# Four array tiles for the 47-point products of an FFT, mixing and feed-forward kernel on one core: units in doubles, a shared ring of PSUM banks, other distances between operands

## The chip, the cores and the metric

One core of a Trainium2 chip. The metric is the device time of one launch in microseconds (us). The kernel before takes 2804.76 us, the median of 3 runs from 2804.42 to 2804.91.

## What is computed

```python
X = np.fft.rfft(x, axis=1)                      # x: 8 x 3008 x 256, float32
Yr = Xr @ w_r - Xi @ w_i + b_r                  # w_r, w_i: 256 x 256
Yi = Xr @ w_i + Xi @ w_r + b_i
Y = soft(Yr) + 1j * soft(Yi)                    # sign(v) * max(|v| - 0.01, 0)
y = np.fft.irfft(Y, n=3008, axis=1)
gate = sigmoid(y @ w_gate)                      # 24064 tokens, 256 -> 1536
out = (gate * (y @ w_val)) @ w_out              # 1536 -> 256
```

## The kernel before

The length 3008 is 47 times 64. The forward transform of a sequence has two steps. Step A is a 47-point product over the rows, with the table `fa` as stationary operand. It goes out to the DRAM tensor `zd`, and step B reads `zd` back for a 64-point product (`fwd_b`, tile `pb`). Then come mixing (`mix`, tiles `pm` and `pm3`), the soft threshold and the inverse 64-point product (`inv_b`, tile `pi`), whose result goes to DRAM as `vd`. The inverse of step A (`load_v`, `inv_a`, tile `pia`) is the 47-point product back: here the data `vf` is stationary and the table `fb_sb` moves.

Step A takes two rows of the 64 at once: `fa` holds the 47-point table twice, interleaved, so that one matmul contracts 94 partitions into 96 (`product_a`, tile `pa`). A call of `fwd_a` handles 4 column positions of both halves with two matmuls of 512 columns. The inverse does the same with 96 partitions and 94 moving columns: a unit `u` is four matmuls. There are 128 units, 16 in each of 8 sequences, and `fwd_a` or its half-sized form `half_a` covers the 16 matmuls of a sequence. These products, step B and the table products of the first sequence are plain float32. The trace shows each such matmul as two weight loads and two matmuls; the order of the program shows it once. The rest splits its operands into two float32r parts, with three matmuls for a product.

The feed-forward part is direct for the first 9 blocks of 512 tokens: `ffn1` makes `pg` and `pv` with 12 matmuls each step, `ffn2` makes `po` with 6. It uses `yth`, `ytl`, `hh` and `hl` as moving operands and `w1h`, `w1l`, `w2` as stationary ones. All later tokens are written to DRAM as `yd`, and 19 pairs of blocks of 512 go through a Strassen scheme: `half` makes seven products in the banks `pa` to `pd` (line 661), four of which open a bank and three of which add to one, and `second` makes 12 matmuls into `po` between them (lines 636 to 638).

Four stages follow each other: the transform of sequence 0 and the start of 1 (to 100 us), the first direct block beside the weights' conversion and step A of sequences 2 and 3 (to 185 us), the other eight direct blocks with all the rest of the transforms merged in (to 1064.5 us), and the Strassen scheme. In the third stage the unit lists in `side` are dealt out between the steps of `ffn`, by weights that stand for TensorE time (1.7 for a `fwd_a`, 0.65 for an inverse unit); a scheduler then sets the order on each engine. Sequences 4 to 7 have step A there (`step_a` in `fft_units`), and 122 of the 128 inverse units are run there. PSUM's eight banks are 3 for the transforms (`FFT_BANKS`), 3 for `ffn1` (`L1_BANKS`) and 2 for `po`.

Of the kernel before, what the change touches and what calls it, by code (L numbers as in the profile page):

```python
# [27 lines left out]
FFT_BANKS, L1_BANKS, L2_BANKS = 3, 3, 2  # L28

NF2K, NR2K, NLD, NST, NBIG, NMF, NME, NVF, NVO, NHH, NSG, NYF = 5, 4, 3, 3, 5, 3, 2, 3, 1, 3, 2, 3  # L30
# [4 lines left out]
PRE = 2  # L35
# [30 lines left out]
def _tables(seq):  # L66
# [3 lines left out]
    fa = np.zeros((R2, 2, NK2, 2, 2))  # L70
    fb = np.zeros((NK2, 2, 2, 128))
    for j in range(2):
        fa[:, j, :, 0, j] = c
        fa[:, j, :, 1, j] = -s
        fb[:, 0, j, j:2 * R2:2] = c.T / seq
        fb[:, 1, j, j:2 * R2:2] = -s.T / seq
    fa = fa.reshape(2 * R2, 2 * NQ)
    fb = fb.reshape(2 * NQ, 128).astype(np.float32)
# [27 lines left out]
    return {"mf": mf, "mi": mi, "mis": mis, "fa": fa.astype(np.float32), "fb": fb}  # L106
# [3 lines left out]
def tile_fft_mix_ffn(ctx: ExitStack, tc, x, w_r, w_i, b_r, b_i, w_one, w_out, mf, mi, mis, fa, fb, out):  # L110
# [9 lines left out]
    PT = 2 * R2  # L120
    UT = 2 * PT
    NU = B * H // 2
# [9 lines left out]
    edge.tile([P, 8], F32, name="edge")  # L132
# [6 lines left out]
    psl = ctx.enter_context(tc.tile_pool(name="psl", bufs=3, space=bass.MemoryType.PSUM))  # L139
    psfs = ExitStack()  # L140
    psf = psfs.enter_context(tc.tile_pool(name="psf", bufs=FFT_BANKS, space=bass.MemoryType.PSUM))

    def bank(name, tag="fft", bufs=FFT_BANKS):
        return (psf if tag == "fft" else psl).tile([P, 512], F32, tag=tag, bufs=bufs, name=name)
# [7 lines left out]
    fa_sb = cw.tile([2 * R2, 2 * NQ], F32, name="fa_sb")  # L152
# [9 lines left out]
    vv = [v.rearrange("q (j h) c -> (q j) h c", j=2) for v in vd]  # L162
# [18 lines left out]
    def fwd_a(b, h):  # L181

        xf = held["x", b, h]
        for i in range(2):
            at = slice(2 * i, 2 * i + 2)
            product_a(xf[:2 * R2, at], xf[:2 * NQ, at], nc.vector.tensor_copy if b < 2 and i else nc.scalar.copy)
# [9 lines left out]
    def half_a(b, h):  # L196

        xi = held.pop(("xh", b, h))[:2 * R2]
        az = p2.tile([P, 2, D], F32, tag="st", bufs=NST, name="azh")[:2 * NQ]
        product_a(xi, az, nc.scalar.copy)  # L200
        nc.gpsimd.dma_start(zv[b][:, 2 * h:2 * h + 2], az)


# [5 lines left out]
    def load_mi(q, full, later=False):  # L209
        t = p2.tile([P, 2, 2, P], F32 if full else F32R, tag="mi_sb", bufs=NME, name="mi_sb")  # L210
        if full:
# [16 lines left out]

    def load_b(b, q):
# [91 lines left out]
    def load_v(u):  # L321
        own = 2 * UT <= u * UT < T0
        vf = p3.tile([P, 2, D], F32, tag="vo" if own else "vf", bufs=NVO if own else NVF, name="vf")[:2 * NQ]
        b, h = divmod(2 * u, H)
        nc.sync.dma_start(vf, vv[b][:, h:h + 2])
        held["v", u] = vf
# [3 lines left out]
    def split_y(c, at, n, y):  # L330
        if c not in yts:
            yts[c] = [p3.tile([P, CT, CW], F32R, name=t) for t in ("yth", "ytl")]
# [4 lines left out]
    def inv_a(u):  # L337
        vf = held.pop(("v", u))
        pa = bank("pia")[:, :CT * UT].rearrange("p (c h k) -> p c h k", c=CT, h=2)
# [3 lines left out]
        py = pa.rearrange("p c h k -> p c (h k)")  # L343
        lo = u * UT
        n = 0
        if lo < T0:
            c, at = divmod(lo, CW)
            n = min(UT, CW - at)
        if 0 < n < UT and lo + n < T0:
            t = p3.tile([P, 3 * P], F32, name="carry", bufs=1)[:, :CT * UT].rearrange("p (c k) -> p c k", c=CT)[:, :, :UT - n]  # L350
            nc.scalar.copy(t, py[:, :, n:])
            held["carry", c + 1] = t, UT - n
        if n:
            split_y(c, at, n, py[:, :, :n])
        if lo + UT > T0:
            t = result("yf")
            t = t[:, :CT * (UT - n)].rearrange("p (c k) -> p c k", c=CT)
            nc.scalar.copy(t, py[:, :, n:])
            nc.sync.dma_start(yd[:, :, lo + n - T0:lo + UT - T0], t)
# [3 lines left out]

    def carry(c):
        if ("carry", c) in held:
            t, n = held.pop(("carry", c))
            split_y(c, 0, n, t)

# [26 lines left out]
    def ffn1(c, f):  # L395
        yth, ytl = yts[c]
        pg, pv = bank("pg", "l1", L1_BANKS), bank("pv", "l1", L1_BANKS)
# [44 lines left out]
    def fft_units(bs, ms):  # L442


        aa = [(b, h) for b in bs for h in range(R1 // 8)]
        units = []

        def step_a(i):
            if i == 0:
                for k in range(min(PRE, len(aa))):  # L450
                    load_a(*aa[k])
            if i + PRE < len(aa):
                load_a(*aa[i + PRE])
            fwd_a(*aa[i])
            store_a(*aa[i])
# [23 lines left out]
        first = [(1.7, lambda i=i: step_a(i)) for i in range(len(aa))]  # L479
# [6 lines left out]
    def ffn_units():  # L486
# [3 lines left out]
        def own(c):  # L490

            return range(-(-c * CW // UT), -(-(c + 1) * CW // UT))

        for c in range(1, NPL):
            at = (c - 1) * NF
            for i, u in enumerate(own(c)):
                todo.setdefault(at + (0, 3, 6)[i], []).append(lambda u=u: load_v(u))
                todo.setdefault(at + (3, 6, 9)[i], []).append(lambda u=u: inv_a(u))
            todo.setdefault(at + 1, []).append(lambda c=c: carry(c))

        def unit(n):
            c, f = seq[n]
            if n == 0:
                for i, u in enumerate(own(0)):
                    if i == 1:
                        w = w1h[:, 0].rearrange("p i t n -> p (i t n)")
                        keep_warm(bank("warm", "l1", L1_BANKS), w[:, :P], w, WARM_V)
                    inv_a(u)
# [160 lines left out]
    def half(k, extra):  # L669
# [76 lines left out]
    ebias = cw.tile([P, 16], F32, name="ebias")[:, :1]  # L746
    fb_sb = const.tile([2 * NQ, P], F32, name="fb_sb")
# [113 lines left out]
    with tc.manual_schedule():  # L861
# [22 lines left out]
        for q in range(NP + 2):  # L884
# [7 lines left out]
            if q == 3:  # L892
                nc.sync.dma_start(fb_sb, fb)
# [58 lines left out]
    def inverse(g):  # L952

        us = [u for b in g for u in range(b * H // 2, (b + 1) * H // 2) if u >= u0]
# [10 lines left out]
        return [(0.0, begin)], [(0.65, lambda i=i: go(i)) for i in range(len(us))]  # L965
# [26 lines left out]
    for j in range(NF, len(ffn)):  # L992
# [5 lines left out]
        while side and (acc >= side[0][0] or j >= (part if len(side) > n_last else end) - 1):  # L998
# [12 lines left out]
            if not side:  # L1011
                psfs.close()
                psg = ctx.enter_context(tc.tile_pool(name="psg", bufs=1, space=bass.MemoryType.PSUM, reuse_waits="tile"))
# [16 lines left out]

    open_banks(0)
    first_product = products(0)
    a, b, c, d = banks[0]
    for o, xn, wn in (a, "a11", "b11"), (d, "s3", "t3"), (b, "s2", "t2"), (c, "s1", "t1"):
# [61 lines left out]
```

## Time and profile before

| | us |
|---|---|
| median of 3 runs | 2804.76 |
| span of the profiled execution | 2802.9 |
| TensorE (PE) matmuls, busy | 2786.4 (99%) |
| PE weight loads, busy | 2304.7 (82%) |
| VectorE (DVE) | 2084.6 (74%) |
| ScalarE (ACT) | 1311.1 (47%) |
| GpSimd (POOL) | 713.1 (25%) |

The profiled execution's own time is not listed apart from its span; the median lies 1.9 us above the span, which holds what goes on before the first and after the last instruction. A busy time is the union of the durations of an engine's instructions. Matmuls overlap each other in the array, so the duration of one is longer than the distance from its start to the start of the next, and only the latter says what a matmul costs in a stream.

### The profile page before, as it was taken

The numbers are of one execution on the slowest core, as the hardware profiler recorded it, in microseconds if no ns is written. First come the engines' busy times: TensorE is split into PE (matmuls) and PEld (weight loads), VectorE is DVE, ScalarE is ACT, GpSimd is POOL, SyncE is SP. The second block draws the span as 40 slices with busy tenths as digits, with TensorE's granted clock in tenths as the row PEclk, the third lists the DMA queues.
The fourth block names the chain that finished last, engine by engine and source line by source line (L and its number), as shares of the span: only waits on it lengthen the run. The fifth ranks groups of instructions, "written<-read, shape, count | busy, mean of one in ns | idle before, by whom it ended". The sixth has DMA issues, their size and how long they took to land.

```text
span 2802.9 us, 38251 instructions
## 1 busy us (share of the span) xinstructions
PE 2786.4 (99%) x13896; PEld 2304.7 (82%) x13896; DVE 2084.6 (74%) x3109; ACT 1311.1 (47%) x2276; POOL 713.1 (25%) x638
## 2 busy tenths in 40 slices
PE   9999999999999999999999999999999999999999
PEld 6778888888899888888888888888888888888887
DVE  5777788767787536777777777777777777777776
ACT  4664544545455444444444444444444444444443
POOL 0211010224100002333433333333333243333321
PEclk9999999999999999999999999999999999999999
DMA  9866545666554661000000000000000000000000
GB/s 296 258 216 193 172 144 151 199 186 193 168 153 144 187 188 36 31 16 16 31 31 28 3 31 31 31 16 16 31 31 16 15 31 31 31 2 30 31 16 16
DMA packets 173469, 241.01 MB, mean 86 GB/s; under 512 B 14592, under 2 KB 124896, under 8 KB 173280
## 3 DMA queue, kind: packets, MB, share of 16 engines
q1 hardware_dynamic: 163776, 214.93, 25.2%
q0 software_dynamic: 9408, 23.60, 2.6%
q8 instruction: 110, 1.80, 0.3%
q14 instruction: 79, 0.65, 0.1%
q10 hardware_dynamic: 96, 0.04, 0.0%
HBM read 134.17 MB, written 104.33 MB: 85 GB/s over the span
## 4 chain that ended last, share of the span: by engine, by line
PE 96%; DVE 2%; DMA 1%; ACT 0%; issue 0%; SPq 0%; DVEq 0%; ACTq 0%
PE pd L661 11%; PE pa L661 11%; PE pc L661 11%; PE po L636 8%; PE po L638 7%; PE po L637 7%; PE pm L273 6%; PE pb L661 5%; PE pia L342 4%; PE pa L178 3%; PE pb L239 3%; PE pg L401 2%; PE pg L403 2%; PE pg L402 2%; PE po L429 2%; PE pv L401 2%
## 5 line engine op out<-in xcount | busy, mean ns | idle before, releaser
L636 PE MATMUL po<-hh,w 128*128 128x512 f32 x912 | 360.1, 395 | 0.0
L638 PE MATMUL po<-hl,w 128*128 128x512 f32 x912 | 358.0, 393 | 0.0
L720 POOL TENSOR_TENSOR c<-c,c 128x512 f32<-128x512 f32 x114 | 148.3, 1301 | 820.8 <-DVE c L716 630.7
L637 PE MATMUL po<-hh,w 128*128 128x512 f32 x912 | 355.9, 390 | 0.0
L661 PE MATMUL pa<-a,w1h 128*128 128x512 f32 x912 | 284.0, 393 | 0.0
L661 PE MATMUL pc<-s,w1h 128*128 128x512 f32 x912 | 282.6, 391 | 0.0
L716 DVE TENSOR_TENSOR c<-u,pc 128x512 f32<-128x512 f32 x228 | 156.8, 688 | 106.3 <-PE pc L661 99.1
L691 DVE TENSOR_TENSOR u<-u,pb 128x512 f32<-128x512 f32 x228 | 155.4, 681 | 90.5 <-PE pb L661 63.5
L608 ACT CAST hh<-v 128x512 fp32r<-128x512 f32 x114 | 70.8, 621 | 305.9 <-DVE v L701 305.9
L638 PEld LDWEIGHTS po<-hl,w 128*128 128x128 f32 x912 | 171.0, 188 | 41.0
L661 PEld LDWEIGHTS pc<-s,w1h 128*128 128x128 f32 x912 | 171.1, 188 | 38.6
L637 PEld LDWEIGHTS po<-hh,w 128*128 128x128 f32 x912 | 171.2, 188 | 38.3
L661 PEld LDWEIGHTS pa<-a,w1h 128*128 128x128 f32 x912 | 171.3, 188 | 37.5
L636 PEld LDWEIGHTS po<-hh,w 128*128 128x128 f32 x912 | 171.3, 188 | 36.8
L612 POOL TENSOR_TENSOR hl<-c,hh 128x512 fp32r<-128x512 f32 x114 | 153.1, 1343 | 186.2 <-ACT hh L608 186.2
L273 PE MATMUL pm<-w_sb,xsh 128*128 128x256 f32 x1008 | 187.0, 286 | 1.7 <-ACT xf L179 1.2
L661 PE MATMUL pa<-a,w1l 128*128 128x512 f32 x456 | 179.2, 393 | 0.0
L661 PE MATMUL pc<-s,w1l 128*128 128x512 f32 x456 | 178.3, 391 | 0.0
L722 DVE TENSOR_TENSOR u<-u,pd 128x512 f32<-128x512 f32 x228 | 156.8, 688 | 24.5 <-DVE c L716 0.9
L695 DVE TENSOR_TENSOR v<-v,pc 128x512 f32<-128x512 f32 x228 | 156.7, 687 | 24.5 <-PE po L638 0.5
L693 DVE TENSOR_TENSOR v<-u,pd 128x512 f32<-128x512 f32 x228 | 156.8, 688 | 24.0 <-DVE u L691 0.5
L687 ACT COPY u<-pa 128x512 f32<-128x512 f32 x228 | 133.7, 586 | 77.0 <-PE pa L661 76.8
(174 smaller groups left out, 6738.2 us busy)
## 6 DMA issues: line engine op xcount, KB each, us to landing
zf<-zd SPq DMA_DIRECT2D x96, 256.0 KB, 3.6
vf<-vd SPq DMA_DIRECT2D x128, 192.0 KB, 3.2
out_dram<-ot SPq DMA_DIRECT2D x93, 256.0 KB, 2.2
vd<-vz SPq DMA_DIRECT2D x84, 256.0 KB, 2.9
ypair<-yd SPq DMA_DIRECT2D x19, 1024.0 KB, 5.0
yd<-yf SPq DMA_DIRECT2D x103, 188.0 KB, 3.2
xf<-in_x_dram SPq DMA_DIRECT2D x48, 384.0 KB, 4.2
zd<-xf SPq DMA_DIRECT2D x44, 384.0 KB, 3.5
```

Of the source, the lines that this page charges most:

```text
L273: nc.tensor.matmul(o, l, r, start=(i == 0), stop=(i == len(mms) - 1))
L612: sub_(hl, h, hh)
L636: nc.tensor.matmul(o, wh, hh, start=(f == 0), stop=False)
L637: nc.tensor.matmul(o, wl, hh, start=False, stop=False)
L638: nc.tensor.matmul(o, wh, hl, start=False, stop=(f == NF - 1))
L661: nc.tensor.matmul(o, l, r, start=not more and l is wh and r is xh, stop=l is wl, skip_group_check=more)
L691: add(u, u, b)
L693: add(v, u, d)
L695: add(v, v, c)
L716: add(c12, u, c)
L720: nc.gpsimd.tensor_mul(c12, g12, c12)
L722: add(u, u, d)
```

## The change

- **Forward step A of sequences 4 to 7** (`load_d`, `fwd_d` in place of `load_a`, `fwd_a`, `store_a`). The host lays the two halves of the 64 rows at partitions 0 to 46 and 64 to 110. One double handles 8 of the former column positions: two tiles `xd`, and 8 matmuls of 47 partitions by 64 stationary columns by 512 moving columns. Each runs on a quarter of the array, rows 0 or 64 and columns 0 or 64, in the order of the four quarters, twice. The product's output is the same amount of data; a sequence has 4 such doubles instead of 8 calls. Loads and stores are 4 each per double (48 partitions) instead of 2 each (96 partitions and over).
- **Inverse units** (`load_v`, `inv_a`) in doubles: 64 units instead of 128. A double is 32 matmuls of 48 partitions by 64 stationary columns by 47 moving columns, in turn on the four quarters, into two banks (one for each half of the rows). Parts that cross a block of 512 tokens are split in place; the `carry` copies are gone, and `yth`, `ytl` have three buffers.
- **PSUM**: the transforms and `ffn1` share one ring of 6 banks (`RING`). The Strassen part opens its own 6 after the operands of the first pair are prepared.
- **Strassen order**: in `half` the product with `s1` (into `c`) comes before that with `s3` (into `d`).
- **Addresses**: unused tiles (`gap`, a larger `edge`, padded small tables) and a smaller scratch for DMA descriptors move the operands. Distances from the start of the stationary to that of the moving operand, in bytes modulo 512, as both programs place them: `hh`, `yth` to `w2`, `w1h` 320 before (64 modulo 128), 480 after (96 modulo 128). Step B 0 before, 448 after. `inv_b` 0 before, 448 after. Mixing 448 both times. The Strassen products, with the operands `a11` to `s4`, 0 both times.

```diff
-FFT_BANKS, L1_BANKS, L2_BANKS = 3, 3, 2
+RING, L1_BANKS, L2_BANKS = 6, 3, 2
...
+    def fwd_d(b, h):
+        ts = held.pop(("xd", b, h))
+        for i in range(2):
+            at = slice(2 * i, 2 * i + 2)
+            os = [bank("pd") for _ in range(2)]
+            for c in range(2):
+                for r in range(2):
+                    rows = slice(64 * r, 64 * r + R2)
+                    in_turn(nc.tensor.matmul(os[r][64 * c:64 * c + 64], ft_sb[rows, :64], ts[c][rows, at],
+                                             start=True, stop=True), i or c or r)
+            for r in range(2):
+                nc.scalar.copy(ts[r][:, at], os[r].rearrange("p (h c) -> p h c", h=2))
...
     def load_b(b, q):
+        gap(16)
...
-    def inv_a(u):
+    def inv_a(u, ordered=False):
-        for hh in range(2):
-            for ct in range(CT):
-                nc.tensor.matmul(pa[:, ct, hh], vf[:, hh, ct * P:(ct + 1) * P], fb_sb[:, :PT], start=True, stop=True)
+        for ct in range(CT):
+            for h in range(4):
+                for c in range(2):
+                    for r in range(2):
+                        rows = slice(64 * r, 64 * r + NQ)
+                        at = ct * P + 64 * c
+                        in_turn(nc.tensor.matmul(os[r][64 * c:64 * c + 64, ct, h], vf[rows, h, at:at + 64],
+                                                 ft_sb[rows, 64:64 + R2], start=True, stop=True), not (first or ordered))
...
-        first = [(1.7, lambda i=i: step_a(i)) for i in range(len(aa))]
+        first = [(2.1, lambda i=i: step_a(i)) for i in range(len(aa))]
...
+        product1(c, "s1", "t1")
+        add(v, u, c)
         product1(d, "s3", "t3")
-        add(v, u, d)
-        product1(c, "s1", "t1")
-        add(v, v, c)
+        add(v, v, d)
...
-        return [(0.0, begin)], [(0.65, lambda i=i: go(i)) for i in range(len(us))]
+        return [(0.0, begin)], [(1.2, lambda i=i: go(i)) for i in range(len(us))]
```

Two places show the new order on PE, both in the third stage. First, before: a unit of the inverse (`pia`) and a call of `fwd_a` (`pa`, two matmuls) between the matmuls of the direct block.

```order
L403 MATMUL pv<-yth,w1l 128x512
L342 MATMUL pia<-fb_sb,vf 128x94 x4
L429 MATMUL po<-hh,w_107 128x512
L430 MATMUL po<-hh,w_107 128x512
L431 MATMUL po<-hl,w_107 128x512
L429 MATMUL po<-hh,w_107 128x512
L430 MATMUL po<-hh,w_107 128x512
L431 MATMUL po<-hl,w_107 128x512
L178 MATMUL pa<-xf,fa_sb 96x512 x2
L342 MATMUL pia<-fb_sb,vf 128x94 x4
L401 MATMUL pg<-yth,w1h 128x512
```

With the change: a double of the inverse behind the inverse 64-point product, ahead of the next step of `ffn1`.

```order
L350 MATMUL pi<-yh,mi_sb 128x256
L388 MATMUL pia<-ft_sb,vf 64x47 x32
L441 MATMUL pg<-yth,w1h 128x512
L442 MATMUL pg<-ytl,w1h 128x512
L443 MATMUL pg<-yth,w1l 128x512
```

And with the change: a double of the forward step A (`pd`, eight matmuls) between `ffn2` and `ffn1`.

```order
L470 MATMUL po<-hh,w_107 128x512
L471 MATMUL po<-hl,w_107 128x512
L224 MATMUL pd<-xd,ft_sb 64x512 x8
L441 MATMUL pg<-yth,w1h 128x512
L442 MATMUL pg<-ytl,w1h 128x512
```

What moved: four small matmuls on the whole array have become 32 on quarters of it for twice the work, and two calls of two have become one run of eight. In the whole program 81 such runs on quarters, `pia`, `pd` or both, stand between matmuls on the whole array.

## Rows read from the trace of the kernel before

**Rows 1.** The page: span, and busy time of each engine.
```profile
span 2802.9 us, 38251 instructions
PE 2786.4 (99%) x13896; PEld 2304.7 (82%) x13896; DVE 2084.6 (74%) x3109; ACT 1311.1 (47%) x2276; POOL 713.1 (25%) x638
```
**Rows 2.** The four stages: length, busy time of each engine (and its instructions), granted PE clock, share of the DMA engines, GB/s.
```profile
0.00:100.00 100.00, 94.07 (x523) 71.22 (x524) 66.80 (x115) 50.17 (x91) 10.81 (x19) 1.00 0.89 273
100.00:185.00 85.00, 83.66 (x328) 57.07 (x326) 56.82 (x99) 55.42 (x101) 20.43 (x37) 0.98 0.87 273
185.00:1064.50 879.50, 875.00 (x5505) 761.85 (x5504) 621.18 (x1070) 431.85 (x741) 108.01 (x156) 1.00 0.58 171
1064.50:2803.00 1738.50, 1733.71 (x7546) 1414.52 (x7544) 1339.76 (x1826) 773.71 (x1346) 573.86 (x426) 1.00 0.07 23
```
**Rows 3.** What PE waited for in the third stage, all of it, and below in the fourth: us in total, times, longest.
```profile
PE pm L273 <- ACT xf L179: 1.2, 1, 1.2
PE pi L310 <- ACT yh L284: 0.9, 3, 0.3
PE pia L342 <- DVE ys L279: 0.8, 2, 0.6
PE pi L310 <- ACT yf L358: 0.6, 1, 0.6
PE pm L273 <- DVE ys L279: 0.5, 1, 0.5
PE pia L342 <- ACT xsf L251: 0.3, 1, 0.3
...
PE pd L661 <- DVE u L722: 0.4, 1, 0.4
```
**Rows 4.** Groups of PE by line and shape: count | busy us, mean ns of one | idle before.
```profile
L636 PE MATMUL po<-hh,w 128*128 128x512 f32 x912 | 360.1, 395 | 0.0
L342 PE MATMUL pia<-fb_sb,vf 96*128 96x94 f32 x1024 | 130.1, 273 | 1.9 <-DVE ys L279 0.8 <-DMA vf<-vd 0.7 <-ACT xsf L251 0.3
L178 PE MATMUL pa<-xf,fa_sb 94*96 94x512 f32 x192 | 89.8, 598 | 2.1 <-ACT xf L179 1.1 <-DVE xf L179 0.8
L401 PE MATMUL pg<-yth,w1h 128*128 128x512 f32 x216 | 99.6, 461 | 0.6 <-ACT yth L334 0.6
```
**Rows 5.** PE in order of time: start us, us, engine, line, instruction, shape, how many in a row. Two units of the inverse between two matmuls of the direct block.
```profile
987.80 0.40 PE L431 MATMUL po<-hl,w 128*128 128x512 f32 x1
988.03 1.92 PE L342 MATMUL pia<-fb_sb,vf 96*128 96x94 f32 x16
989.74 0.48 PE L401 MATMUL pg<-yth,w1h 128*128 128x512 f32 x1
990.05 0.40 PE L402 MATMUL pg<-ytl,w1h 128*128 128x512 f32 x1
990.29 0.39 PE L403 MATMUL pg<-yth,w1l 128*128 128x512 f32 x1
```
**Rows 6.** The same view: a call of `fwd_a` in the third stage.
```profile
337.64 1.88 PE L178 MATMUL pa<-xf,fa_sb 94*96 94x512 f32 x4
339.36 1.01 PE L342 MATMUL pia<-fb_sb,vf 96*128 96x94 f32 x7
```
**Rows 7.** Weight loads of the two kinds of product: ns least/median/most, first and last start.
```profile
L342 PEld LDWEIGHTS pia<-fb_sb,vf x1024: 186/192/193, 101.0 to 1053.9; 96*128 96x128 f32 x171
L178 PEld LDWEIGHTS pa<-xf,fa_sb x128: 159/162/166, 207.6 to 722.3; 94*96 94x96 f32 x128
```
**Rows 8.** PE in order of time: eight loads and matmuls of 128 stationary and 128 moving columns (step B).
```profile
701.38 1.05 PE L239 MATMUL pb<-mf_sb,zf 128*128 128x128 f32 x8
702.19 0.48 PE L273 MATMUL pm<-w_sb,xsh 128*128 128x256 f32 x2
```
**Rows 9.** PE in order of time: two starts that lie close together.
```profile
390.07 0.59 PE L178 MATMUL pa<-xf,fa_sb 94*96 94x512 f32 x1
390.09 0.79 PE L401 MATMUL pg<-yth,w1h 128*128 128x512 f32 x1
```
**Rows 10.** PE in order of time in the Strassen part: the start of the three products that add to a bank with the first that opens one, of the others, and of `second`.
```profile
1499.88 0.62 PE L661 MATMUL pc<-s,w1h 128*128 128x512 f32 x2
...
1501.95 0.62 PE L661 MATMUL pb<-s,th 128*128 128x512 f32 x2
...
1503.99 0.40 PE L636 MATMUL po<-hh,w 128*128 128x512 f32 x1
1504.22 0.40 PE L637 MATMUL po<-hh,w 128*128 128x512 f32 x1
1504.46 0.39 PE L638 MATMUL po<-hl,w 128*128 128x512 f32 x1
1504.69 0.39 PE L636 MATMUL po<-hh,w 128*128 128x512 f32 x1
...
1506.07 0.39 PE L636 MATMUL po<-hh,w 128*128 128x512 f32 x1
```

**Rows 11.** The page: one of DVE's sums in the Strassen part (count | busy us, mean ns | idle before), and the loads of x (count, KB each, median us to landing).
```profile
L693 DVE TENSOR_TENSOR v<-u,pd 128x512 f32<-128x512 f32 x228 | 156.8, 688 | 24.0 <-DVE u L691 0.5
...
xf<-in_x_dram SPq DMA_DIRECT2D x48, 384.0 KB, 4.2
```

More of the change, by code (lines that the diff above doesn't have):

```diff
@@ L227, in keep_mi, with gap @@
         kept.add(q)
+    gaps = set()
+    def gap(n):
+        if n not in gaps:
+            gaps.add(n)
+            p2.tile([P, n], F32, name=f"gap{n}", bufs=1)
     def load_b(b, q):
+        gap(16)
         zf = p2.tile([P, 2, D], F32, tag="ld", bufs=NLD, name="zf")
@@ L321, in load_v @@
     def load_v(u):
[L322 to L325, printed above, removed]
+        own = 4 * UT <= 2 * u * UT < T0
+        vf = p3.tile([P, 4, D], F32, tag="vo" if own else "vf", bufs=NVO if own else NVF, name="vf")
+        b, h = divmod(u, H // 4)
+        for r in range(2):
+            n1 = 32 * r + 4 * h
+            nc.sync.dma_start(vf[64 * r:64 * r + NQ], vd[b][:, n1:n1 + 4])
         held["v", u] = vf
@@ L335, in split_y @@
         sub(yl, y, yh)
-    def inv_a(u):
+    def inv_a(u, ordered=False):
         vf = held.pop(("v", u))
-        pa = bank("pia")[:, :CT * UT].rearrange("p (c h k) -> p c h k", c=CT, h=2)
-        for hh in range(2):
-            for ct in range(CT):
-                nc.tensor.matmul(pa[:, ct, hh], vf[:, hh, ct * P:(ct + 1) * P], fb_sb[:, :PT], start=True, stop=True)
[L343 to L359, printed above, removed]
+        os = [bank("pia")[:, :CT * UT].rearrange("p (c h k) -> p c h k", c=CT, h=4) for _ in range(2)]
+        first = True
+        for ct in range(CT):
+            for h in range(4):
+                for c in range(2):
+                    for r in range(2):
+                        rows = slice(64 * r, 64 * r + NQ)
+                        at = ct * P + 64 * c
+                        in_turn(nc.tensor.matmul(os[r][64 * c:64 * c + 64, ct, h], vf[rows, h, at:at + 64],
+                                                 ft_sb[rows, 64:64 + R2], start=True, stop=True), not (first or ordered))
+                        first = False
+        for r in range(2):
+            py = os[r].rearrange("p c h k -> p c (h k)")
+            lo = (2 * u + r) * UT
+            end = lo + UT
+            at = lo
+            while at < end:
+                if at >= T0:
+                    t = result("yf")[:, :CT * (end - at)].rearrange("p (c k) -> p c k", c=CT)
+                    nc.scalar.copy(t, py[:, :, at - lo:])
+                    nc.sync.dma_start(yd[:, :, at - T0:end - T0], t)
+                    break
+                c = at // CW
+                n = min(end, (c + 1) * CW) - at
+                split_y(c, at - c * CW, n, py[:, :, at - lo:at - lo + n])
+                at += n
@@ L442, in fft_units @@
     def fft_units(bs, ms):
-        aa = [(b, h) for b in bs for h in range(R1 // 8)]
+        aa = [(b, h) for b in bs for h in range(0, R1 // 8, 2)]
         units = []
@@ L450, in step_a @@
                 for k in range(min(PRE, len(aa))):
[L451 removed]
+                    load_d(*aa[k])
             if i + PRE < len(aa):
[L453 to L455 removed]
+                load_d(*aa[i + PRE])
+            fwd_d(*aa[i])
         def loads(q, b):
@@ L952, in inverse @@
     def inverse(g):
-        us = [u for b in g for u in range(b * H // 2, (b + 1) * H // 2) if u >= u0]
+        us = [u for b in g for u in range(b * H // 4, (b + 1) * H // 4) if u >= u0]
         ahead = min(NVF - 1, len(us))
```

101 lines of the change are left out of this document (53 added, 48 removed).

## Prediction, made before the run

> **What bounds the kernel now.** I read the page first: PE has matmuls in flight 99% of the span and no other engine comes near it [rows 1]. A full row could still hide waiting, so the next view is the busy time by stage: PE is full in each, at the full clock (0.98 to 1.00), with DVE at 71% and DMA at 58% in the third stage [rows 2]. The third view is what PE waited for. In the third stage it adds up to 4.4 us of 879.5, in the fourth to 0.4 us of 1738.5 [rows 3]. So the time is a sum of matmuls, and a change is worth what it takes out of PE's stream. The number that counts is the distance from one start to the next, not the duration: a 512-column matmul lasts 0.39 us but the next one starts 0.23 us later [rows 5].
>
> **Inverse units.** The 1024 records of `pia` are 128 units of 8 [rows 4]. Two units run from 988.03 to 989.74, 1.71 us; the matmul behind them then holds the stream for 0.31 us instead of 0.23, so the pair costs 1.79 us [rows 5]. That is 0.107 us a record, although 94 moving columns were streamed. Step B streams 128 columns and needs about the same, (702.19 - 701.38)/8 = 0.101 [rows 8]. The common part is a load of 128 stationary columns, so the load sets the pace. Loads of 96 columns last 162 ns, of 128 columns 192 ns [rows 7]: time goes with columns.
>
> A double of the change has 32 products, so 64 loads and matmuls: 16 rounds of the four quarters. If a quarter's load of 64 columns lasts half as long and the four go side by side, a round costs 0.107/2 = 0.054 us. Moving 47 columns is half of 94, and those fitted under 0.107. The double is then 16 x 0.054 = 0.86 us. To it I add the change of shape. No row shows the array change from whole to quarters. From below it costs nothing. From above, each side waits for the old matmul to leave and for a load that nothing covers: 0.39 - 0.23 = 0.16 us of tail and 0.19 us of load, 0.35 us, twice a run [rows 5, 7]. I take the tail alone, 2 x 0.16 = 0.33 us, since loads run ahead of matmuls everywhere in this trace. The double costs 1.19 us against 1.79: 64 x 0.60 = **38 us less**. Ends with the shape at nothing and at 0.70: 0.86 and 1.56, so 60 less to 15 less.
>
> [...]
>
> **Forward step A of sequences 4 to 7.** A call of `fwd_a` takes 339.36 - 337.64 = 1.72 us for 4 records, 0.43 each, set by 512 columns [rows 6]. Four sequences have 32 calls, so 16 doubles replace 16 x 3.44 = 55 us. A double has 8 products, 16 records: 4 rounds of the four quarters at 0.43, as each quarter still streams 512 columns, plus 0.33 for the shape: 2.05 us. That is 16 x 1.39 = **22 us less** (ends 27 and 16 with the shape at nothing and at 0.7).
>
> **Addresses.** Products with operands at distance 0 run 9 matmuls in 1503.99 - 1501.95 = 2.04 us, 0.2267 each; the `second` block, at 64 modulo 128, runs 6 in 1506.07 - 1504.69 = 1.38 us, 0.230, with 0.24 once near its start [rows 10]. The direct blocks have the same 64 and the same 0.23 [rows 5]. There are 3 x 912 matmuls in `second` [rows 4] and 9 x 216 in the direct blocks, 4680 in all; each nanosecond is 4.7 us. The new distance, 96 modulo 128, is in no row. It lies between 64 and the next 0, so I take half of the 3.3 ns: **8 us less**. If they go at 0.2267 and the nine products behind `second`, which now take 0.230 (1499.88 to 1501.95, 2.07 us) [rows 10], do too, it is 6732 x 3.3 ns = 22 less. If they all go at 0.235, 23 more. Step B, mixing and `inv_b`: no price, since the loads set their pace at distances 0 and 64 alike [rows 5, 8].
>
> **The ring of banks.** It can take away part of the 4.4 us of waits [rows 3]: **2 less**, ends 4 less and 4 more, since a slow eviction of the transforms now also holds banks that `ffn1` had for itself.
>
> **Costed at nothing.** The swap of `s1` and `s3`: DVE's sums come in another order, under the 12 matmuls of `second` (12 x 0.23 = 2.8 us against 0.69 for a sum [rows 10, 11], and PE waits 0.4 us in that stage in all [rows 3]). Evictions: the same number of ACT copies, eight `carry` copies fewer; ACT is busy 49% of the third stage [rows 2]. DMAs: the x loads and `zd` stores of four sequences become twice as many of half the size on SP's queue, and with `PRE = 1` a load is issued one step ahead; 32 calls now lie between 207.6 and 722.3 us [rows 7], so a double is due every 32 us, and a load of x lands after 4.2 [rows 11]. If that cover went, PE would wait at `pd`, by some 4 us a double. After the change DVE has 621 us in some 815, so no engine overtakes PE.
>
> **The sum.** 38 + 22 + 8 + 2 = 70 us less than the profiled execution's 2802.9 us of span and the 1.9 us between span and median: 2804.8 - 70 = **2735 us**.
>
> **Rivals.** *1. The halves of a product stand in each other's way (slower).* Each product is two records, and both belong to the same quarter, one right behind the other. If matmuls start strictly in order, the second half waits for the first, and everything behind it waits too; then only the second half of one product overlaps with the first half of the next. A double of the inverse is 32 x 0.054 + 0.33 = 2.06 us, 0.27 over 1.79, 17 us more. A forward double is 8 x 0.43 + 0.43 + 0.33 = 4.20, 0.76 over 3.44, 12 us more. With 10 less from addresses and ring: 2804.8 + 17 + 12 - 10 = 2824 us. It decides once a round of four quarters costs more than (1.79 - 0.33)/16 = 0.091 us in the inverse and 0.78 us in the forward products. For it: in every row the halves follow each other, never overlapping by more than the tail. Against: no row has two quarters.
> [...]
>
> *2. The forward products overlap, the short ones do not get loaded fast enough.* If loads go two at a time, an inverse double is 2.06 us as above, 17 more, and the forward part stays 22 less: 2804.8 + 17 - 22 - 10 = 2790 us. For it: the inverse is bound by loads already. Against: two starts can lie 20 ns apart [rows 9], so issue allows 64 in 1.3 us.
> [...]
>
> *3. The quarters take turns.* Then the change doesn't do what it says. Rounds cost 4 x 0.054 and 4 x 0.43: a double of the inverse 3.8 us, 2.0 more, a forward one 7.2 us, 3.8 more: 128 + 60 - 10, about 2983 us.
>
> *4. The addresses bring the most they can.* The forecast with 22 less from addresses and 4 from the ring: 2719 us; with shape changes at nothing (81 runs x 0.33 = 27) down to 2692.
>
> **How the numbers follow.** Forecast 0.62, rival 4 0.10, rival 2 0.12, rival 1 0.12, rival 3 0.04. Rows speak for the forecast's parts (load time goes with columns, stream time with columns, PE is all there is), and what no row shows is whether quarters overlap, which the three rivals share. The forecast's own range is 2705 (shape free) to 2775 (shape at 0.7 us a run, 81 x 0.37 = 30, and addresses at 10 more than taken). The range 2690 to 2800 adds rivals 2 and 4; rivals 1 and 3 and a little at either end are left out, 0.2 in all. A measurement of this kernel tells apart about 0.2%, 5.6 us. Faster: the forecast, rival 4 and 0.08 of rival 2, 0.80. Within: 0.03 of rival 2. Slower: rivals 1 and 3 and the rest, 0.17.
>
> **What would show it.** In the profile after: `pia` has 4096 records, `pd` 256; a run of 64 `pia` followed by `pg` should take 1.2 us from its first start to the stream's resuming, a run of 16 `pd` about 2.0. Over 1.8 and 3.4 the quarters don't pay. Starts of consecutive records on different quarters would lie 10 to 20 ns apart in the forecast, and on the same quarter 0.43 us apart in `pd`. The distance between starts in `second` would be 0.227 to 0.230. The third stage would shrink from 879.5 to about 820, the fourth from 1738.5 by 3 to 16. The prediction is wrong if PE shows waits of over 10 us in the third stage, if a shape change costs over 0.7 us a run, or if the Strassen part gets longer.

## The result, and the profile after

| | before | after |
|---|---|---|
| median of 4 runs, us | 2804.59 | 2759.1 |
| least to most | 2803.27 to 2804.91 | 2757.48 to 2764.2 |
| ratio, 95% interval | | 0.9842 [0.9828, 0.9856] |

The change saves 45.5 us. That is inside the range, and 65% of the 70 us in the sum. The profiled execution took 2758.12 us, its span 2756.2. Three executions of the experiments below, one each of e6, e7 and e10, ran at a granted clock of 0.56 to 0.85, took 3041 to 4560 us and are left out.

First the page of the changed kernel: span, and busy time of each engine, as in [rows 1].

```profile
span 2756.2 us, 44624 instructions
PE 2735.6 (99%) x17096; PEld 2241.2 (81%) x17096; DVE 2080.7 (75%) x3109; ACT 1291.2 (47%) x2268; POOL 712.3 (26%) x638
```

PE has 3200 more instructions (3072 `pia` and 128 net of `pa` and `pd`) and is busy for 51 us less. It is still the bound. Next the four stages, columns as in [rows 2].

```profile
0.00:100.00 100.00, 94.44 (x527) 71.44 (x527) 67.44 (x115) 51.24 (x93) 12.00 (x22) 1.00 0.89 278
100.00:185.00 85.00, 82.09 (x470) 54.88 (x471) 56.17 (x98) 53.29 (x96) 18.95 (x35) 0.98 0.89 272
185.00:1020.00 835.00, 826.76 (x8571) 700.80 (x8570) 621.58 (x1072) 416.05 (x736) 110.03 (x156) 1.00 0.62 181
1020.00:2756.00 1736.00, 1732.33 (x7534) 1414.06 (x7532) 1335.48 (x1825) 770.63 (x1344) 571.29 (x426) 1.00 0.06 23
```

The third stage has shrunk from 879.5 us to 835, and the fourth has hardly moved. PE's time without a matmul rose from 16.5 us of the span [rows 1] to 20.6 (2756.2 - 2735.6), in the third stage from 4.5 (879.5 - 875.0) [rows 2] to 8.2 (835.0 - 826.8). The longest waits of PE in the third stage name where (us in total, times, longest), against [rows 3]; all of them add up to 8.0 us there, where they were 4.4:

```profile
PE pi L348 <- ACT yh L322: 2.2, 5, 1.1
PE pia L388 <- DMA vf<-vd: 1.1, 3, 0.6
PE po L469 <- ACT hh L457: 1.1, 1, 1.1
PE pia L388 <- ACT sg L447: 1.0, 1, 1.0
```

Now the runs on quarters. PE in order of time (start us, us, engine, line, instruction, shape, how many in a row): a double of the inverse.

```profile
502.74 0.28 PE L349 MATMUL pi<-yl,mi_sb 128*128 128x256 f32 x1
502.86 0.28 PE L350 MATMUL pi<-yh,mi_sb 128*128 128x256 f32 x1
503.06 1.15 PE L388 MATMUL pia<-ft_sb,vf 48*64 48x47 f32 x64
504.14 0.50 PE L441 MATMUL pg<-yth,w1h 128*128 128x512 f32 x1
504.48 0.40 PE L442 MATMUL pg<-ytl,w1h 128*128 128x512 f32 x1
504.71 0.40 PE L443 MATMUL pg<-yth,w1l 128*128 128x512 f32 x1
```

The same view, a double of the forward step A:

```profile
343.12 0.28 PE L350 MATMUL pi<-yh,mi_sb 128*128 128x256 f32 x1
343.33 1.95 PE L224 MATMUL pd<-xd,ft_sb 47*64 47x512 f32 x16
345.21 0.50 PE L441 MATMUL pg<-yth,w1h 128*128 128x512 f32 x1
345.55 0.40 PE L442 MATMUL pg<-ytl,w1h 128*128 128x512 f32 x1
```

Each run is read by three distances. Ahead of the inverse double the last `pi` holds the stream for 0.20 us (502.86 to 503.06) instead of the usual 0.11. The double lasts 1.08 us to the next start. The first `pg` then holds 0.34 us instead of 0.235. In all it costs 0.09 + 1.08 + 0.11 = 1.28 us, where two units cost 1.79 [rows 5]. By the same reading the forward double costs 0.10 + 1.88 + 0.11 = 2.09 us, against 3.44, which is two calls of 1.72 [rows 6]. Both are typical: most of the 81 runs have these lengths to 0.01 us.

The times from start to start, added up by tile over the whole trace, show where the 46 us of the profiled executions lie (a shape change counts partly with the neighbour of the run, and a wait with the matmul ahead of it):

| us | before | after | |
|---|---|---|---|
| `pia`, `pa`, `pd` | 212.8 | 162.3 | -50.5 |
| `pg`, `pv`, `po` of the direct blocks | 469.0 | 474.5 | +5.5 |
| `pb`, `pm`, `pi`, `warm` | 385.9 | 383.8 | -2.1 |
| `second` | 629.7 | 638.7 | +9.0 |
| Strassen products | 1099.5 | 1091.2 | -8.3 |

Where they don't wait, the new products give nearly what was expected of them. What failed is the address part: `second` became slower. Its rows, as in [rows 10]:

```profile
1502.27 0.40 PE L674 MATMUL po<-hh,w 128*128 128x512 f32 x1
1502.50 0.40 PE L675 MATMUL po<-hh,w 128*128 128x512 f32 x1
1502.74 0.40 PE L676 MATMUL po<-hl,w 128*128 128x512 f32 x1
1502.97 0.40 PE L674 MATMUL po<-hh,w 128*128 128x512 f32 x1
...
1504.37 0.40 PE L674 MATMUL po<-hh,w 128*128 128x512 f32 x1
```

Nine starts in 2.10 us are 0.233 each, against 0.230 before [rows 10].

### The profile page after: what moved, and what is told of

The parts are those of the page before. It is cut to its first block, busy times and chain, and to the rows that moved or that the text cites. A ratio compares the mean times of both kernels' runs of the same rounds, so it can differ in the third digit from the quotient of the medians.

```text
span 2756.2 us, 44624 instructions
## 1 busy us (share of the span) xinstructions
PE 2735.6 (99%) x17096; PEld 2241.2 (81%) x17096; DVE 2080.7 (75%) x3109; ACT 1291.2 (47%) x2268; POOL 712.3 (26%) x638
## 4 chain that ended last, share of the span: by engine, by line
PE 92%; DVE 4%; DMA 1%; issue 1%; ACT 1%; SPq 0%; POOL 0%; DVEq 0%; ACTq 0%; POOLq 0%
PE pa L699 11%; PE pc L699 11%; PE pd L699 11%; PE po L675 8%; PE po L674 8%; PE po L676 8%; PE pb L699 6%; PE pm L311 5%; PE pb L277 3%; PE pia L388 2%; PE pg L441 2%; PE po L469 2%; PE pv L441 1%; PE pv L442 1%; PE pv L443 1%; PE po L470 1%
## 5 line engine op out<-in xcount | busy, mean ns | idle before, releaser
L731 DVE TENSOR_TENSOR v<-u,pc 128x512 f32<-128x512 f32 x228 | 156.9, 688 | 24.4 <-PE pd L699 0.5
L733 DVE TENSOR_TENSOR v<-v,pd 128x512 f32<-128x512 f32 x228 | 156.7, 687 | 24.4 <-DVE v L731 0.9
```

The source lines that it names most:

```text
L731: add(v, u, c)
L733: add(v, v, d)
```

## The experiments

Medians stand beside the kernel before on the same chip; ratios are to that kernel, with 95% intervals. A float of `edge` more takes 4 bytes off the distance of `hh` and `yth` to their weights; it moves some other operands too. The weights `w1h`, `w1l` and `w2` start at 128 modulo 512 in all these programs, and only the moving operand moves. So these runs can't tell its distance to the weights from its own address; "distance" below stands for either.

### e1: the change with distance 0

```diff
-    edge.tile([P, 96], F32, name="edge")
+    edge.tile([P, 88], F32, name="edge")
```

> The changed kernel with the tile `edge` 32 bytes smaller, so that the moving operands of the direct blocks and of `second` lie at distance 0 modulo 512 from their weights instead of 480; nothing else. Theory A (the distance sets the spacing, and 0 is what gives the Strassen products 0.2267 us): the spacing in `second` falls from 0.234 to 0.227, in the direct blocks from 0.234 to 0.228, so (2736 + 1944) x 0.007 = 33 us less than the changed kernel, about 2726 us. Rival B (the spacing comes from switching banks and from the order of the three matmuls, not from addresses): 0.234 stays and the time is within 3 us of 2759.

Measured: 2734.53 us (2732.21 to 2735.64), before 2804.89, ratio 0.9751 [0.9735, 0.9767]. `second` takes 226.7 ns a matmul, 619.9 us in all, the products 226.8 and 1085.8. So 32 bytes of padding are worth 25 us; 33 were expected. `second` brings 18.8 of them and the products 5.4. So the spacing follows the addresses and not the banks or the order of the three matmuls: rival B is out.

### e2: the change with the old distance, 320

```diff
-    edge.tile([P, 96], F32, name="edge")
+    edge.tile([P, 8], F32, name="edge")
```

> The changed kernel with `edge` as it was before, so that those operands lie at distance 320 modulo 512, as in the kernel before; nothing else. Theory A: the pattern 0.232, 0.226, 0.229 comes back in `second` and in the direct blocks, 4680 x 0.004 = 19 us less, and the transient of the accumulating products behind `second` costs about 25 ns more each half, 228 x 0.025 = 6 us more: about 2746 us. Rival B: within 3 us of 2759.

Measured: 2753.32 us (2751.18 to 2756.63), 0.9821 [0.9807, 0.9836]; `second` 230.3 ns (629.8 us), the products 229.1 (1097.0). The old spacing is back, and with it the slower products behind `second`. The new distance costs the change 5.8 us, where 13 were expected with the products' gain already taken off: `second` has 9.0 us of the expected 11, but the direct blocks only 2.3 of 8 (474.5 to 472.2).

### e3: the change with distance 256

```diff
-    edge.tile([P, 96], F32, name="edge")
+    edge.tile([P, 24], F32, name="edge")
```

> The changed kernel with the distance of those operands at 256 modulo 512 (0 modulo 128). Theory A in the form that only the distance modulo 128 counts: as at distance 0, 0.227 in `second`, about 2726 us. Theory A in the form that the distance modulo 512 counts: another spacing than at 0, between 0.227 and 0.235, so 2726 to 2763 us. Rival B: within 3 us of 2759.

Measured: 2730.46 us (2725.84 to 2735.08), 0.9739 [0.9723, 0.9755]. `second` takes 226.7 ns and the products 226.8, the same as at 0. PE in the Strassen part of this kernel, in order of time:

```profile
1505.02 0.39 PE L674 MATMUL po<-hh,w 128*128 128x512 f32 x1
1505.25 0.39 PE L675 MATMUL po<-hh,w 128*128 128x512 f32 x1
1505.47 0.39 PE L676 MATMUL po<-hl,w 128*128 128x512 f32 x1
1505.70 0.39 PE L674 MATMUL po<-hh,w 128*128 128x512 f32 x1
...
1507.06 0.39 PE L674 MATMUL po<-hh,w 128*128 128x512 f32 x1
```

Nine starts in 2.04 us: 0.2267. This version beats both kernels, the change by 28.6 us.

### e4: the kernel before with the new distance, 480

```diff
-    edge.tile([P, 8], F32, name="edge")
+    edge.tile([P, 96], F32, name="edge")
```

> The kernel before with `edge` as in the change, so that the direct blocks and `second` get distance 480 modulo 512 there; nothing else. Theory A: `second` goes from 0.230 to 0.234 and the direct blocks likewise, 4680 x 0.004 = 19 us more, the products behind `second` 228 x 0.025 = 6 us less: about 2818 us. Rival B, and the theory that the slower spacing comes from the ring of banks or the new order of the Strassen products: within 3 us of 2804.6.

Measured over 10 runs: 2809.49 us (2807.72 to 2811.96), before 2804.89, 1.0018 [1.0009, 1.0028]. `second` goes from 230.2 to 233.5 ns (+8.9 us) and the direct `pv` from 230.3 to 234, as forecast. The products fall from 1099.5 to 1094.0 us and the median start distance of `pm` from 118 to 114 ns, which was not forecast; most of the operands of `pm` have not moved. So the distance alone is slower, by less than the 13 us expected.

### e5: one quarter after the other

```diff
-        for ct in range(CT):
-            for h in range(4):
-                for c in range(2):
-                    for r in range(2):
+        for c in range(2):
+            for r in range(2):
+                for ct in range(CT):
+                    for h in range(4):
```

> The changed kernel with the 32 products of an inverse double in another order: the eight of one quarter of the array, then the eight of the next, instead of the quarters in turn; same work. Theory S (the gain comes from quarters that work side by side, and it needs neighbours in the stream to be on different quarters): a double is 64 records at the pace of one load of 64 columns, 64 x 0.058 + 0.34 = 4.1 us instead of 1.28, 64 x 2.8 = 177 us more, about 2936 us. Rival T (the gain comes from shorter loads and streams, the order is free, or PE finds the next quarter's work by itself): 1.28 us a double as now, 2759 us.

Measured: 2917.75 us (two runs, 2913.96 and 2921.55), before 2804.49, 1.0403 [1.0382, 1.0424]. A `pia` record takes 53.1 ns instead of 18.8, 217.7 us in all instead of 77.2. A double in this kernel, PE in order of time:

```profile
533.95 0.28 PE L350 MATMUL pi<-yh,mi_sb 128*128 128x256 f32 x1
534.16 3.31 PE L388 MATMUL pia<-ft_sb,vf 48*64 48x47 f32 x64
537.40 0.50 PE L441 MATMUL pg<-yth,w1h 128*128 128x512 f32 x1
```

It lasts 3.24 us instead of 1.08; with its ends, 4.1 were expected. On one quarter the records start 0.058 us apart, the two halves of a product as well. Eight of them, four products, in 0.45 us (length, busy time and instructions of PE and PEld):

```profile
534.15:534.60 0.45, 0.44 (x8) 0.44 (x8) 0.00 (x0) 0.00 (x0) 1.00 0.04 11
```

Only the next quarter's first records start ahead of their turn: the first at 534.886, beside the 13th of the quarter before (534.880), whose last three follow at 534.938, 534.996 and 535.055. This overlap, three times in a double, is what makes it shorter than 64 x 0.058 = 3.7 us. In the change's order a round of four records on four quarters takes the same 0.058 us as one record here. So the gain of the inverse hangs on the order of the quarters. The stages of this kernel show a second price (the third stage up to 1040 us of its end at 1182):

```profile
100.00:185.00 85.00, 82.28 (x428) 59.09 (x429) 51.81 (x92) 48.19 (x86) 17.83 (x32) 0.90 0.80 241
185.00:1040.00 855.00, 853.93 (x7265) 746.05 (x7264) 596.94 (x1035) 389.86 (x669) 103.60 (x157) 0.97 0.53 156
```

The granted clock was 0.90 and 0.97 in the mean where the change has 0.98 and 1.00. In the third stage it fell again and again while PE was full and ran such doubles, to 0.80 between 760 and 780 us and to 0.83 between 880 and 900. So not all of the 159 us over the change is the order itself; `pia` has 140 of them.

### e6: one more change of shape in each double

```diff
-        os = [bank("pia")[:, :CT * UT].rearrange("p (c h k) -> p c h k", c=CT, h=4) for _ in range(2)]
+        bs = [bank("pia") for _ in range(2)]
+        os = [b[:, :CT * UT].rearrange("p (c h k) -> p c h k", c=CT, h=4) for b in bs]
         first = True
         for ct in range(CT):
+            if ct:
+                wx = w1h[:, 0, 0, 0]
+                in_turn(nc.tensor.matmul(bs[0][:, 384:], wx, wx, start=True, stop=True), not ordered)
```

The added matmul writes columns that nobody reads.

> The changed kernel with one more matmul on the whole array (128 x 128, into unused columns of the double's first bank) in the middle of each inverse double, so that the array changes shape four times in a double instead of two. Theory D (a change of shape there and back costs what a double shows over its 8 rounds of 0.117 us: 0.10 ahead, 0.14 inside, 0.11 behind, 0.35 us together): 64 x (0.35 + 0.11 for the matmul itself) = 29 us more than the changed kernel, about 2788 us. Rival (the 0.35 us is the start of the pipe after other work and has little to do with the shape): 64 x 0.11 = 7 us more, about 2766 us.

Measured: 2783.33 us (2780.07 to 2784.99), before 2804.49, 0.9922 [0.9905, 0.9938]: 24 us over the change. PE in order of time:

```profile
507.08 0.68 PE L392 MATMUL pia<-ft_sb,vf 48*64 48x47 f32 x32
507.69 0.33 PE L386 MATMUL pia<-w1h 128*128 128x128 f32 x1
507.95 0.68 PE L392 MATMUL pia<-ft_sb,vf 48*64 48x47 f32 x32
508.56 0.50 PE L445 MATMUL pg<-yth,w1h 128*128 128x512 f32 x1
```

The double takes 1.48 us instead of 1.08; over all 64 the sum of `pia` grows by 23.2 us, 0.36 each. That is the price of one change there and back with a small matmul in it, for which 0.46 were expected, 0.11 of them for the matmul. So the change alone costs at most 0.36 us, and 0.25 if the matmul costs its 0.11; the 0.33 that was taken lies between. It also sizes a round: 32 records take 0.61 us and 64 take 1.08, so 32 more cost 0.47, or 0.059 for each four.
The change of shape, at 0.36 us at most there and back, is half of the 0.70 us at the upper end of the forecast.

### e7: banks apart again

```diff
-    psf = psfs.enter_context(tc.tile_pool(name="psf", bufs=RING, space=bass.MemoryType.PSUM))
+    psf = psfs.enter_context(tc.tile_pool(name="psf", bufs=3, space=bass.MemoryType.PSUM))
...
-        pg, pv = bank("pg"), bank("pv")
+        pg, pv = bank("pg", "f1"), bank("pv", "f1")
```

> The changed kernel with three banks for the transforms and three for ffn1 as before, instead of the ring of six. Theory R0 (PE's waits on banks were small before, the ring is worth 0 to 4 us): 2759 to 2763 us. Rival R1 (the ring is what lets the doubles, which need two banks at once, run without a wait): PE's waits in the third stage grow by 20 us or more, 2780 us or above.

Measured: 2807.54 us (2803.22 to 2810.71), before 2804.49, 1.0009 [0.9999, 1.0018]. The whole gain is gone, 48 us. Its third stage up to 1040 us, the two longest of PE's waits in the whole run, and one forward double:

```profile
185.00:1040.00 855.00, 839.16 (x8295) 691.47 (x8294) 616.24 (x1060) 411.80 (x721) 109.62 (x159) 1.00 0.60 173
```

```profile
PE pd L224 <- ACT xd L227: 4.3, 9, 0.8
PE pia L388 <- DMA vf<-vd: 4.2, 5, 1.9
```

```profile
357.00 3.59 PE L224 MATMUL pd<-xd,ft_sb 47*64 47x512 f32 x16
360.52 0.50 PE L441 MATMUL pg<-yth,w1h 128*128 128x512 f32 x1
```

The forward double lasts 3.52 us instead of 1.88. It needs two banks, and then two more, and with three it waits for ACT's copy in its middle (nine such waits, 4.3 us in all). PE is without a matmul for 15.8 us of this stage, and over the whole run the sum of `pd` grows from 33.7 to 54.0 us, that of `pg` from 161.6 to 173.9. So the ring is no small part of its own: the doubles need it.

### e8: without the gaps

```diff
-        if n not in gaps:
+        if False:
```

This puts step B, mixing and `inv_b` at distance 0 modulo 512.

> The changed kernel without the two unused tiles in the transforms' pool, so that step B, mixing and inv_b have distance 0 modulo 512 instead of 448; the direct blocks and second keep 480. Theory A0 (a multiple of 128 is best for every shape): the 256-column matmuls come at 113 ns instead of 116.6, (1512 + 504) x 0.003 = 6 us less, 2753 us. Rival A1 (for matmuls that load as long as they stream, 448 is better, as the lower median of mixing and inv_b after the change suggests): 4 to 8 us more, about 2765 us. Rival A2 (loads set the pace, distance does nothing there): within 3 us of 2759.

Measured: 2766.7 us (2764.84 to 2767.85), 0.9863 [0.9846, 0.9879], 7.6 us over the change. The median start distance of `pm` and of `pi` goes from 114 to 120 ns. The change's gaps are worth 7.6 us that the sum had put at nothing; for these matmuls of 256 columns 448 is better than 0 here (114 ns against 120), while for 512 columns 0 and 256 were the best (226.7 ns, e1 and e3). Only the stationary operands were moved, so the moving operand's own address can't be the cause. But 448 alone doesn't give 114: in the kernel before `pm` stood there too, at 118.

### e9: the kernel before with distance 256

```diff
-    edge.tile([P, 8], F32, name="edge")
+    edge.tile([P, 24], F32, name="edge")
```

> The kernel before with `edge` 64 bytes larger, so that the direct blocks and second have distance 256 modulo 512 (0 modulo 128) instead of 320; nothing else. Theory A (a distance that is a multiple of 128 gives 0.2267 us a matmul, and the Strassen products behind second lose their slow start with it): second 2736 x 0.0035 = 10 us, products 4788 x 0.0028 = 13 us, direct blocks 1944 x 0.003 = 6 us, 29 us less than the kernel before, about 2776 us. Rival (the addresses only matter together with the doubles, the ring or the new order): within 3 us of 2804.6.

Measured: 2784.54 us (2783.43 to 2785.87), before 2804.44, 0.9929 [0.9914, 0.9944]. One number in the kernel before is worth 20 us; 29 were expected. `second` takes 226.8 ns (620.2 us), as in e3, but the products only come to 228.0 (1091.6 us), not to 226.8.

### e10: the kernel before with the ring

```diff
-FFT_BANKS, L1_BANKS, L2_BANKS = 3, 3, 2
+FFT_BANKS, L1_BANKS, L2_BANKS = 6, 3, 2
...
-        pg, pv = bank("pg", "l1", L1_BANKS), bank("pv", "l1", L1_BANKS)
+        pg, pv = bank("pg"), bank("pv")
```

The Strassen banks open later, as in the change.

> The kernel before with a ring of six banks for the transforms and ffn1 in place of three and three, and the Strassen part's own banks opened behind the preparation of its first pair, as in the change; products, units and addresses as before. Theory R (the ring is worth what PE waits for, and the 48 us lost without it in the changed kernel come from the doubles, which take two banks at once): 2800 to 2806 us. Rival (ffn1 and the transforms gain from sharing banks by themselves): 2790 us or less.

Measured: 2796.79 us (2794.51 to 2799.59), before 2804.44, 0.9973 [0.9961, 0.9985], 7.7 us less. It falls between the two expectations. The third stage, to 1060:

```profile
185.00:1060.00 875.00, 873.69 (x5519) 764.76 (x5518) 622.86 (x1073) 431.34 (x742) 107.35 (x156) 1.00 0.58 172
```

PE's time without a matmul falls from 4.5 us to 1.3. That is 3.2 of the 7.7. By tile, `pia` and `pa` lost 4.3 us (212.8 to 208.5), and `pb`, `pm`, `pi` and `warm` 3.5 (385.9 to 382.4): the gain lies with the transforms, not with `ffn1`.

### e11: the old order of s1 and s3

```diff
-        product1(c, "s1", "t1")
-        add(v, u, c)
         product1(d, "s3", "t3")
-        add(v, v, d)
+        add(v, u, d)
+        product1(c, "s1", "t1")
+        add(v, v, c)
```

> The changed kernel with the product of s3 ahead of that of s1 again, in half and in the products that open the Strassen part; nothing else. By all theories nothing hangs on it but DVE's order of two sums: within 3 us of 2759. If the shorter slow start of the products behind second came from the order and not from the distance, the products would rise from 0.2279 to 0.2291, 6 us more.

Measured: 2765.32 us (2761.14 to 2769.09), 0.986 [0.9845, 0.9874], 6.2 us over the change, where at most 3 was expected. In the profiled executions the products take 1094.1 us instead of 1091.2, and the Strassen part starts 6.6 us later, which the swap can't cause directly. The granted clock differs ahead of it: 0.74 against 0.91 from 100 to 120 us, 0.98 against 1.00 from 800 to 1000. The executions in which it was 0.999 on average took 2761.14 us here and 2757.48 and 2758.12 in the change. So about 3 us are the swap, and the rest goes with the clock.

### e12: the change with distance 32

```diff
-    edge.tile([P, 96], F32, name="edge")
+    edge.tile([P, 80], F32, name="edge")
```

> The changed kernel with the direct blocks and second at distance 32 modulo 512. Theory A measured 0.2267 us at 0 and 256, 0.2302 at 320 (64 modulo 128) and 0.2335 at 480 (96 modulo 128). If the spacing depends on how far the moving operand lies past a multiple of 128, and rises with it, 32 gives 0.228 to 0.229, 4680 x 0.005 = 23 us less than the changed kernel, about 2740 us. If it depends on the distance to the nearest multiple of 128 (32 and 96 alike), it gives 0.2335 and 2759 us.

Measured: 2766.38 us (2763.39 to 2770.5), 0.9865 [0.985, 0.9879]; `second` 233.6 ns (638.9 us), the products 228.5 (1094.0). PE in order of time:

```profile
1503.02 0.40 PE L674 MATMUL po<-hh,w 128*128 128x512 f32 x1
...
1504.42 0.39 PE L674 MATMUL po<-hh,w 128*128 128x512 f32 x1
```

Six starts in 1.40 us are 0.233 each: 32 is as bad as 480. So the spacing does not rise with how far the distance lies past a multiple of 128: at 32 past one (32, 233.6 ns) and 96 past one (480, 233.5 ns) it is alike, and at 64 past one (320, 230.3 ns) it is shorter than at both. Of the 7.3 us over the change the products have 2.8 and `pm` 1.9 (218.0 to 219.9); the rest was not settled.

## Why the prediction was right, and where its sum was not

**The mechanism.** The quarters work side by side, so that rivals 1 to 3 are out: e5 shows what the inverse costs where they don't, 3.24 us a double against 1.08. For the forward doubles no run changes the order; 16 records in 1.88 us, four times 0.43 and a shape change, is what the trace has for them. `pia` has 4096 records and `pd` 256, as foretold:

```profile
L388 PEld LDWEIGHTS pia<-ft_sb,vf x4096: 129/135/228, 99.9 to 1006.4; 48*64 48x64 f32 x196
L388 PE MATMUL pia<-ft_sb,vf x4096: 223/232/318, 99.9 to 1006.5; 48*64 48x47 f32 x196
```

**Inverse, 38 forecast.** Loads of 64 columns take 0.129 to 0.135 us, two thirds of the 0.192 [rows 7] and not half; the rows had it already, with 0.162 for 96 columns, 84% of 0.192 and not 75%. Four side by side come out at 0.058 to 0.059 a round, where 0.054 was taken. The shape change is 0.09 ahead, 0.14 inside (1.08 - 16 x 0.059) and 0.11 behind, 0.34 in all, where 0.33 was taken. That the two are so near is partly luck, as the forecast had two tails of 0.16 outside the run and nothing inside. A double costs 1.28 us instead of 1.19, so 64 x 0.51 = 33 us.

**Forward, 22 forecast.** 2.09 us a double against 2.05: 16 x 1.35 = 22 us.

**Less than these 55.** In the table the ends of a run count with its neighbours. Without its ends an inverse double should save 1.71 - 1.08 us and a forward double 3.44 - 1.88, 64 x 0.63 + 16 x 1.56 = 65 us in all; the three tiles have 50.5. Nine of the 81 runs are longer than the others of their kind, by 11 us together. The first double is the worst of them. PE in order of time at its place:

```profile
99.94 0.28 PE L388 MATMUL pia<-ft_sb,vf 48*64 48x47 f32 x2 [1.48 <-DMA vf<-vd]
102.43 1.63 PE L388 MATMUL pia<-ft_sb,vf 48*64 48x47 f32 x62 [2.21 <-DMA vf<-vd]
103.99 2.46 PE L876 MATMUL warm<-w1h 128*128 128x512 f32 x5
```

The work ahead of it in PE's order is done by 98.46, and this double waits twice for its loads, 3.7 us in all; it takes 4.0 us to the next start, and `pa` ahead of it holds PE for 1.6 us more than usual. Over the whole run the waits on `vf` grew from 0.7 us [rows 4] to 4.8. The load of a double brings twice as much, and here nothing is ahead of it to hide it. The others wait in their middle, as for `sg` at 940 (1.0 us) and for `yt` at 663 (0.7), or the matmul behind them does, as for `yh` at 706 (1.1). The prediction named this risk for the loads of x alone; those held, no wait of `pd` for `xd` is in the list.

**Addresses, 8 forecast: this step failed.** It put 96 modulo 128 between 64 and the next 0. The runs order them otherwise: 226.7 ns at 0 and 256 (e1, e3), 230.3 at 320 (e2), 233.5 at 480 and 233.6 at 32 (e12). The 0.235 of the upper bound was the nearer end. The new distance costs 5.8 us (e2), and `pm`, whose distance was forecast at no price, gained 3.1 (221.1 to 218.0 us in all). Its distance is 448 in both kernels and e4 brings the same 218.3, so that its own distance is not the cause; what stands around it in the stream may be. So the address part is some 3 us more and not 8 less. The gaps' 7.6 us (e8) are no gain over before in full, since mixing stood at 448 there too. The new distance is also why the Strassen part did not get shorter by 3 to 16: `second` lost 9.0 us, and the products won 8.3. Of these, e4 gets 5.5 from the distance alone and e11 2.9 from the swap.

**The ring, 2 forecast.** As a term of its own it was mis-sized: 7.7 us in the kernel before (e10). It is also what the first two terms stand on (e7, 48 us), which the prediction did not see: it counted the banks as a risk of 4 us. With doubles PE's time without a matmul in the third stage rose by 3.7 us instead of falling, with waits on `yh`, `hh` and `sg` in the list.

**The sum by the runs.** 33 + 22 for the products, 3 for `pm`, 3 for the swap, less 6 for the distance and 13 for the nine longer runs and the `pa` ahead of the first: 42 us, against the 45.5 measured. The 3.5 us between them are not settled; what the ring gives outside the doubles is not in this sum, and the executions of the change alone lie 6.7 us apart, the fastest at a granted clock of 0.999 and the slowest at 0.997. So 2759 us inside the range bears out the first two terms, with e5 and the rows, and not the last two. (The lower end of the forecast's own range, with the shape free, should read 2735 - 27 = 2708 and not 2705.)

**A sign that held, and why rival 1 failed.** "On the same quarter 0.43 us apart in `pd`" is what the records show. The matmuls of the forward double above, in stretches (length, busy time and instructions of PE and PEld, the granted clock third from the end):

```profile
343.30:343.40 0.10, 0.07 (x4) 0.07 (x7) 0.00 (x0) 0.00 (x0) 1.00 0.85 266
343.40:343.75 0.35, 0.35 (x4) 0.14 (x8) 0.00 (x0) 0.00 (x0) 1.00 0.44 132
343.75:343.86 0.11, 0.11 (x8) 0.05 (x4) 0.00 (x0) 0.00 (x0) 1.00 0.24 70
```

Its loads after the first eight come in fours, in order of time:

```profile
343.81 0.15 PEld L224 LDWEIGHTS pd<-xd,ft_sb 47*64 47x64 f32 x4 [0.28 <-ACT xsh L293]
344.24 0.15 PEld L224 LDWEIGHTS pd<-xd,ft_sb 47*64 47x64 f32 x4 [0.28 <-issue]
```

Four records start within 0.02 us, no fifth until 343.81, 0.48 us behind the first, and the next loads lie 0.43 us apart (343.81 to 344.24). The trace does not name a record's quarter. But in the first forward double each of the four products signals its end, and the four signals stand on records 5 to 8. So records 1 to 4 are taken for the first halves, on four quarters, and 5 to 8 for the second halves, 0.48 us later on the same quarters. e5 agrees: on one quarter no two records start together, they lie 0.058 us apart.
Rival 1 had the halves right and what stands behind them wrong. A second half does come behind its first, by 0.43 to 0.48 us, but the products behind it on other quarters start before it; in e5, too, the next quarter's first record starts before the last three of the quarter ahead. The strict order of starts, which rival 1 took as its premise, is not what these traces show.
Within a round of four, neighbouring records start 6 to 7 ns apart, in `pd` and in `pia` (the forecast had 10 to 20), and 64 of `pia` fit in 1.08 us.

## What to carry to other kernels

Price a run on array tiles as rounds times what one record takes from start to start on one tile (here 0.058 us with 47 moving columns in e5, 0.43 with 512 in `pd`), plus the change of shape there and back (0.34 us here, at most 0.36 in e6), and order the products so that neighbours lie on different tiles (1.08 us for a double here, against 3.24 in e5). Before the products are doubled, count the buffers and banks that a double holds at once (three banks in place of the ring cost 48 us here, e7), and look at the first one, which has nothing ahead of it (3.7 us of waits here). For long streams of 512 columns set the distance between stationary and moving operand by a padding tile, and measure it: 0 and 256 bytes modulo 512 were the best of the five distances tried here (226.7 ns, against 230.3 to 233.6), with the weights at 128 modulo 512. That one number was worth 20 us in the old kernel and 28.6 in the new.

## What the runs showed of the hardware

- The start distance of 512-column matmuls in a stream changed with the addresses of their operands: 226.7 ns at a distance of 0 and 256 modulo 512 (e1, e3), 230.3 at 320 (e2), 233.5 at 480 (the change) and 233.6 at 32 (e12), all in `second`. For 256 columns 448 (114 ns) was better than 0 (120 ns) in the change (e8), but mixing at 448 took 118 in the kernel before.
- Float32 records on quarters did not start strictly in the order of the program: in `pd` of the change the first halves of four products start 6 to 7 ns apart and the second halves 0.43 to 0.48 us later; on one quarter records of 47 moving columns start 0.058 us apart (e5).
- The products, at distance 0 themselves, changed with the distance of `second` ahead of them: with the change's order they take 229.1 ns on average at 320 (e2), 227.9 at 480 and 226.8 at 0 and 256 (e1, e3).
- The granted clock was 0.97 in the mean of the third stage up to 1040 us, with PE full, when the quarters were used one after the other (e5), and 0.90 ahead of it (100 to 185 us); with the quarters in turn it was 1.00 and 0.98 in these stages.
